# Attention and MLP on one core: key tiles of 128, a shared block-diagonal tile of 64, and row-tiled AV for the rest keys

## The chip, the cores and the metric

The kernel runs on one core of one Trainium2 chip. The metric is the device time of one execution in microseconds (us); a figure for a kernel is the median of its runs.

Engines are named as the profile names them: PE is TensorE (PEld its weight loads; PEq, SPq and so on are the queues from which an engine takes its instructions), DVE is VectorE, ACT is ScalarE, POOL is GpSimd, SP is SyncE, which issues most DMAs.

## The reference

Attention over 8 batches, 12 heads, 448 positions and head size 64, with RMS-normalised queries and keys, followed by an MLP on the 3584 tokens:

```python
q_n, k_n = rmsnorm(q, g_q), rmsnorm(k, g_k)
scores = (q_n @ k_n.T) / sqrt(64)
attn = softmax(scores)                     # 448 x 448 for each of 96 heads
x = (attn @ v) as [8 * 448, 12 * 64]
h = x @ w_in                               # 768 -> 2048
out = (h * clip(h + 3, 0, 6) / 6) @ w_out  # 2048 -> 768
```

## The kernel before

Two heads make a pair; there are 6 pairs per batch and 48 in all. The program is a list of steps with costs, which a small scheduler puts into a fixed order for each engine. A batch's MLP runs between the attention of the next batch's pairs. Only the first batch has no MLP to fill TensorE with; the *first phase* below is the time until the first MLP matmul.

A pair goes through these stations: loads of k, q and v; squares, a reduction and a reciprocal root (`prep`); scaling into `qks`; a transposition into `kq` and `kp` (`turn`; on TensorE for the first 10 pairs, by DMA later); scores and exponentials (`attend`); AV, the product of the exponentials with v, and its normalisation (`gather`). PSUM is the pool that holds the output tiles of the kernel's matmuls. A head's 448 keys are four tiles of 112:

```python
def heads(src, P):
    b, j = divmod(P, NJ)
    return src[b, 2*j:2*j+2, :, :].rearrange("h (p t) d -> p h (t d)", t=T)   # T = 4, p = 112
# loads: one DMA each for k, q and v of a pair
nc.sync.dma_start(out=vf[0:PT], in_=heads(v, P))

# attend: clusters of two score steps, each two matmuls in half of the array's rows
for t0 in range(0, T, size):                      # size = 1 in the first batch, 2 later
    ...
    nc.tensor.matmul(out=ps[:, a, 0:S], lhsT=kp[rows, c0:c0 + 128], rhs=kq[rows, 1, :], start=True, stop=True)
    ...                                           # then exp on ACT, 112 x 896 values for each step

# gather: 4 query tiles x 2 heads x 4 key tiles of 112
nc.tensor.matmul(out=dst[:, a*E1:(a+1)*E1], lhsT=e[0:PT, t, a, c0:c0 + 128], rhs=va[0:PT, a, t, :], ...)

# the start: the loads of g go out on ACT, after q of the first three pairs
g_load = add("ACT", 2.2, 0, load_g, after=1.5, late=3.0)
```

## Time and profile before

| | before |
|---|---|
| median | 442.24 us (441.35 to 443.99, 4 runs; 442.93 in the three runs known to the prediction) |
| span of the profiled run | 438.6 us |
| PE busy | 410.6 us (94%) |
| DVE, ACT, POOL busy | 246.3, 249.0, 240.2 us |
| first score matmul, first MLP matmul | 14.28, 45.48 us |
| DMA packets | 102,923 |

The busy time of each engine in three stretches, in us; the columns are the stretch, its length, the busy us (with the number of instructions) of PE, PEld, DVE, ACT and POOL, then the granted clock (the share of TensorE's full speed that the chip allowed), the DMA share (the time that all packets took over the time of 16 engines; packets overlap, so it can exceed 1) and GB/s:

```profile
10.00:54.60 44.60, 33.78 (x399) 20.31 (x400) 40.39 (x69) 33.38 (x61) 36.84 (x40) 1.00 1.18 250
54.60:106.00 51.40, 50.66 (x508) 28.40 (x509) 37.17 (x59) 37.09 (x65) 38.95 (x35) 1.00 0.96 207
258.00:308.00 50.00, 49.83 (x449) 27.48 (x450) 27.90 (x48) 29.93 (x52) 32.89 (x29) 1.00 0.63 159
```

The clock column has to be read with care at the start: the trace's records of the clock begin at 25.86 us, and before them the column shows 1.00. The matmuls tell otherwise: two score matmuls take 0.56 us at 24.67 us and 0.36 us at 26.27 us.

The chain of work that ended last, followed back from the last instruction through what released each step, as shares of the span by engine, from the page:

```profile
PE 80%; POOL 5%; DVE 4%; ACT 3%; issue 3%; DMA 3%; SPq 1%; POOLq 0%
```

Last, PE's timeline in the steady phase, with start, duration and operation. Durations overlap, so starts are read: the score cluster (S, x4) starts at 263.69 and the next matmul at 264.17, 0.48 us later.

```profile
263.33 0.42 PE L437 MATMUL R<-va,e 112*128 112x65 bf16 x8
263.69 0.55 PE L416 MATMUL S<-kq,kp 64*128 64x448 bf16 x4
264.17 1.15 PE L533 MATMUL M<-xT,w_in_sb 128*128 128x384 bf16 x6
```

### The profile page before, as it was taken

How to read it: one execution, taken by the hardware profiler on the slowest of the kernel's cores; microseconds unless marked ns; L12 is line 12 of the kernel's file. 1: busy time of each engine (PE TensorE's matmuls, PEld its weight loads, DVE VectorE, ACT ScalarE, POOL GpSimd, SP SyncE). 2: the span in 40 equal slices, each digit the busy share in tenths (PEclk: the TensorE clock that was granted, in tenths of full speed). 3: DMA queues.
4: the chain of work that ended last, by engine and by line, in shares of the span. 5: the costliest groups of instructions: out<-in, count | busy, mean ns of one | idle time of the engine just before them, and what ended most of it. 6: DMA issues, size and time to landing. Idle time of an engine off the chain costs nothing.

```text
span 438.6 us, 9205 instructions
## 1 busy us (share of the span) xinstructions
PE 410.6 (94%) x3663; PEld 229.2 (52%) x3682; DVE 246.3 (56%) x417; ACT 249.0 (57%) x425; POOL 240.2 (55%) x230
## 2 busy tenths in 40 slices
PE   0588799999999999999999999999999999999995
PEld 0355455555455565554455565554455555654563
DVE  1998887657674564456555465556564444334421
ACT  3788588657765666367664677357673665123200
POOL 3499988855757567656765657747757510000000
PEclk9999999999999999999999999999999999999999
DMA  8999999877545745674465655684465420220122
GB/s 241 247 265 261 224 214 193 216 197 192 128 121 148 189 113 136 167 214 111 133 156 157 177 135 145 159 214 109 120 161 164 97 56 12 54 81 0 37 72 73
DMA packets 102923, 64.58 MB, mean 147 GB/s; under 512 B 59744, under 2 KB 99424, under 8 KB 102880
## 3 DMA queue, kind: packets, MB, share of 16 engines
q1 hardware_dynamic: 94544, 57.01, 50.6%
q0 software_dynamic: 7296, 6.29, 9.1%
q10 hardware_dynamic: 1040, 0.69, 0.5%
q8 instruction: 29, 0.48, 0.5%
q14 instruction: 14, 0.11, 0.1%
HBM read 45.61 MB, written 11.01 MB: 129 GB/s over the span
## 4 chain that ended last, share of the span: by engine, by line
PE 80%; POOL 5%; DVE 4%; ACT 3%; issue 3%; DMA 3%; SPq 1%; POOLq 0%
PE M L558 27%; PE M L533 25%; PE S L416 9%; PE X L437 8%; PE S L558 4%; PE R L437 2%; PE S L533 2%; DVE ssq L337 1%; ACT e L421 1%; POOL qks L351 1%; PE X L558 1%; POOL sq L322 1%; POOL va L359 1%; DMA gq_t<-in_g_q_dram 1%; POOL sq L329 1%
## 5 line engine op out<-in xcount | busy, mean ns | idle before, releaser
L421 ACT ACTIVATE e<-S 112x896 bf16<-112x896 f32 x192 | 166.3, 914 | 64.1 <-PE S L416 64.0
L533 PE MATMUL M<-xT,w_in_sb 128*128 128x384 bf16 (+1 forms) x679 | 145.1, 349 | 3.7 <-DVE gT L541 2.9
L351 POOL TENSOR_TENSOR qks<-qk,rs 112x512 bf16<-112x512 f32 x87 | 90.5, 1055 | 86.6 <-ACT rs L344 84.7
L558 PE MATMUL M<-w_out_sb,gT 128*128 128x384 bf16 x736 | 131.8, 326 | 0.0
L558 PEld LDWEIGHTS <-gT 128*128 128x128 bf16 x896 | 82.9, 98 | 57.8 <-issue 7.8
L533 PEld LDWEIGHTS <-w_in_sb 128*128 128x128 bf16 x768 | 69.6, 97 | 67.4 <-issue 12.5
L541 DVE SCALAR_TENSOR_TENSOR gT<-t,M 128x384 bf16<-128x384 f32 (+1 forms) x116 | 70.6, 611 | 59.1 <-ACT t L539 58.3
L539 ACT ACTIVATE t<-M 128x384 f32<-128x384 f32 (+1 forms) x116 | 62.6, 540 | 67.0 <-PE M L533 65.5
L437 PEld LDWEIGHTS <-e 112*128 112x128 bf16 x1536 | 65.1, 99 | 31.4 <-issue 16.0
L337 DVE TENSOR_REDUCE ssq<-sq 112x16 f32<-112x1024 f32 (+1 forms) x49 | 58.4, 1193 | 23.3 <-POOL sq L329 12.2
L329 POOL TENSOR_TENSOR sq<-qk 112x1024 f32<-112x1024 f32 x36 | 68.1, 1892 | 0.0
L416 PE MATMUL S<-kq,kp 64*128 64x448 bf16 x384 | 56.6, 364 | 4.1 <-DVE kp L381 1.7
L437 PE MATMUL X<-va,e 112*128 112x65 bf16 x1152 | 58.6, 196 | 0.8 <-ACT e L421 0.6
L566 DVE COPY y<-M 128x384 f32<-128x384 f32 x46 | 25.6, 556 | 59.2 <-PE M L558 59.0
L359 POOL CAST va<-vf 112x512 bf16<-112x512 f32 x48 | 31.5, 658 | 10.4 <-DMA vf<-in_v_dram 10.1
L392 POOL TENSOR_SCALAR kp<-kq,gp 128x448 bf16<-128x448 bf16 x23 | 32.3, 1402 | 5.3 <-DMA kq<-qks 5.2
L463 DVE TENSOR_TENSOR xn<-X,rd 128x384 bf16<-128x384 f32 x48 | 26.8, 558 | 1.6
L416 PEld LDWEIGHTS <-kp 64*128 64x128 bf16 x384 | 12.2, 94 | 27.7 <-issue 18.0
L437 PE MATMUL R<-va,e 112*128 112x65 bf16 x384 | 20.4, 195 | 0.0
L377 PE MATMUL M<-ident,qks 112*128 112x112 bf16 x80 | 7.9, 242 | 13.0 <-DVE qks L351 12.4
L558 PE MATMUL S<-w_out_sb,gT 128*128 128x384 bf16 x112 | 19.5, 326 | 0.0
L462 DVE RECIPROCAL rd<-X 128x6 f32<-128x6 f32 x48 | 9.2, 192 | 15.3 <-PE X L437 15.2
(42 smaller groups left out, 156.2 us busy)
## 6 DMA issues: line engine op xcount, KB each, us to landing
qk<-in_k_dram SPq DMA_DIRECT2D x48, 224.0 KB, 3.3
vf<-in_v_dram SPq DMA_DIRECT2D x48, 224.0 KB, 3.7
qk<-in_q_dram SPq DMA_DIRECT2D x45, 224.0 KB, 3.4
w_in_sb<-in_moe_w_in_dram POOLq DMA_DIRECT2D x4, 768.0 KB, 11.3
w_out_sb<-in_moe_w_out_dram POOLq DMA_DIRECT2D x4, 768.0 KB, 11.9
out_dram<-y SPq DMA_DIRECT2D x8, 336.0 KB, 3.1
out_dram<-y SPq DMA_DIRECT2D x8, 288.0 KB, 3.4
out_dram<-y SPq DMA_DIRECT2D x8, 240.0 KB, 3.2
```

The source lines that it names most:

```text
L329: parts = [add("POOL", 1.93, at - 10, lambda: nc.gpsimd.tensor_tensor(out=sq[0:PT], in0=qk[0:PT], in1=qk[0:PT], op=MULT), *ld, *war, lock= ...
L337: red = add("DVE", 0.6 * n, at - 8 * hurry + 0.5 * i0, lambda i0=i0, i1=i1, cs=cs: nc.vector.tensor_reduce(out=ssq[0:PT, cs], in_=sq[0:PT, ...
L351: sc.append(add(on, 0, at - 6 * hurry, lambda e, i=i, rs4=rs4: engines[e].tensor_tensor(out=qks[0:PT, i].rearrange("p t h d -> p h t d"), ...
L359: vc = add({"POOL": 0.61}, 0, at - 3, lambda e: engines[e].tensor_copy(out=va[0:PT, :, :, 0:D], in_=vf[0:PT].rearrange("p h (t d) -> p h t ...
L392: nc.vector if e == "DVE" else nc.gpsimd).tensor_scalar_mul(
L416: nc.tensor.matmul(out=ps[:, a, 0:S], lhsT=kp[rows, c0:c0 + 128], rhs=kq[rows, 1, :], start=True, stop=True)
L421: x = add("ACT", 0.93, at + step * (t0 + i) / T + 0.2, lambda t=t0 + i, ps=ps: nc.scalar.activation(out=e[0:PT, t], in_=ps[0:PT, :, 0:S], ...
L437: nc.tensor.matmul(out=dst[:, a * E1:(a + 1) * E1], lhsT=e[0:PT, t, a, c0:c0 + 128], rhs=va[0:PT, a, t, :], start=(first and a == 0 and t ...
L533: nc.tensor.matmul(out=m[:, 0:n], lhsT=w_in_sb[:, kt, f * 128:(f + 1) * 128], rhs=X[:, kt, :], start=(kt == 0), stop=(kt == NKT - 1))
L539: r = add("ACT", 0.08 + n / 1200, due + span, lambda: nc.scalar.activation(out=t[:, 0:n], in_=m[:, 0:n], func=RELU, bias=0.5, scale=1.0 / ...
L541: g = add("DVE", 0.12 + n / 960, due + span, lambda: nc.vector.scalar_tensor_tensor(out=G[:, f, :], in0=t[:, 0:n], scalar=1.0, in1=m[:, 0: ...
L558: nc.tensor.matmul(out=m[:, 0:HALF], lhsT=G[:, f, i * 128:(i + 1) * 128], rhs=w_out_sb[:, f, cols], start=(f == 0), stop=(f == NFT - 1))
```

## The change

The intent is to take work off TensorE. Each head's keys become three tiles of 128 and a rest of 64. The rest keys of both heads lie in one tile of 128 rows (head 0 in the upper half, head 1 in the lower), scaled into a block-diagonal tile, so that one matmul in the full array gives the scores of both heads. From the second batch on two pairs share seven score steps instead of eight. The AV of the rest keys runs in row tiles (64 rows for each head, each head in a part of its own of the PSUM tile `X`) inside a score cluster, and the other AV matmuls fall from 64 to 48 for two pairs. The g loads also go out first. The core of the diff:

```diff
+    K7 = 2 * NS + 1                                     # NS = 3: tiles of 2 heads, and the rest tile
+    def load_tiled(e, at, tile_, src, P, war, cost, after):
+        x = heads(src, P)
+        most = add(e, 0.47, at, lambda: engine.dma_start(
+            out=tile_[:, 0:2 * NS].rearrange("p (h t) d -> p h (t d)", h=2),
+            in_=x[:, 0:SM].rearrange("h (p t) d -> p h (t d)", t=NS)), ...)
+        rest = add(e, 0.47, at, lambda: engine.dma_start(
+            out=tile_[:, 2 * NS], in_=x[:, SM:S]), ...)  # 2 heads x 64 rows of 256 bytes
+        return [most, rest]
 ...
+        def scale_rest():                                # makes the tile block diagonal
+            nc.vector.scalar_tensor_tensor(
+                out=qks[:, NS].rearrange("p (h d) -> p h d", h=2),
+                in0=kf[:, 2 * NS].unsqueeze(1).to_broadcast([128, 2, D]),
+                scalar=rs[:, 2 * NS:2 * NS + 1], in1=head[:], op0=MULT, op1=MULT)
 ...
+                    nc.tensor.matmul(                    # rest keys of AV, in row tiles
+                        out=X[:, a, s * E1:(s + 1) * E1], lhsT=er[rows, i, c0:c0 + 128], rhs=va[rows, 2 * NS, :],
+                        start=(s == 0), stop=False, skip_group_check=True)
 ...
+            for cluster, extra, x in (                   # two pairs, seven steps
+                    ([[(P, NS), (P + 1, NS)]], None, POS[0]),
+                    ([[(P, 2)], [(P + 1, 0)]], (0, P), POS[1]),
+                    ([[(P + 1, 1)], [(P + 1, 2)]], None, POS[2])):
 ...
-    g_load = add("ACT", 2.2, 0, load_g, after=1.5, late=3.0)
+    g_load = add("ACT", 1.95, -99, load_g, after=0.7, late=1.0)
```

Since a shared step needs the keys of the second pair early, `EARLY = 0.7` also moves the preparation of every second pair forward by 0.7 of a pair, from the second batch on.

## The prediction

> **What bounds the kernel now.** TensorE, from about 45 us on. The page's busy table gives PE 410.6 of 438.6 us (94%), and the table by windows gives 49.1 to 49.8 busy us in each stretch of 50 between 158 and 358, clock 1.00. The chain of waits is 80% PE; ACT (57%), DVE (56%) and POOL (55%) are off it there. Before that PE waits, while DVE is busy 40.4 of 44.6 us and POOL 36.8 (windows, 10 to 54.6). The first score matmul starts only at 14.28 us: ACT issues g loads until 8.89 us, although the first keys landed at about 4.2 (timeline, chain).
>
> **What a pair costs PE now** (timeline, start to start, 240 to 275 us). A cluster of two score steps, four matmuls, takes 0.483 us until the next full-array matmul; the change into it adds 0.09 (last AV chunk 0.353 before scores, 0.265 otherwise). [...] Two pairs: 4 x 0.573 for scores, 8 AV chunks x 0.265, together 4.41 us.
>
> **What the change does to that.** Two pairs get three row-tiled clusters (3 x 0.573 = 1.72) and one block-diagonal step of two matmuls in the full array (0.38[...]): scores go from 2.29 to 2.10. AV keeps 48 full matmuls at 0.033 (1.59) and adds 16 row-tiled ones inside existing clusters: 0.26 us if the halves run fully abreast, 0.53 if each costs what it does now; I estimate 0.4. Sum 4.09 against 4.41: 0.32 us per two pairs, 21 times, is 6.7 us (4 to 9.5). All of it is on the critical path.
>
> **The start.** The g loads go out first, q of pair 0 moves to SP. ACT should square at about 5 us and the first scores start at about 10. Afterwards DVE and POOL set the pace with about the same work (reduce 15 instead of 16 groups, key scale 0.55 + 0.26 instead of 0.69, kp 512 instead of 448 columns), so I expect the first MLP matmul at about 42 instead of 45.5 us: 3.5 us (0 to 5).
>
> **What it adds.** k and v take two DMAs each, one with 256-byte rows: 384 packets instead of 224, two more SP issues per pair (0.31 to 0.47 us each; SP has room). kp on POOL grows from 1.40 to about 1.6 us, squares and scales shrink. A score cluster now also waits for X to be free and for the rest keys' exponential: a small new risk of PE stalls, say 0 to 3 us, 0.5 expected.
>
> **Prediction.** 442.9 - 6.7 - 3.5 + 0.5: about 433 us, range 428 to 438.5. Faster by over 2%: 0.58; within 2%: 0.40; slower: 0.02.
>
> **What would show each step.** Score clusters without rest keys still 0.48 us, the block-diagonal pair 0.38 without a gap on either side; clusters with rest keys 0.13 to 0.26 longer. ACT e instructions 168 or so of full size instead of 192. First score at 9 to 11 us, first MLP matmul at 41 to 43. PE busy per 50 us unchanged at 49.5 or more.
>
> **What would make it wrong.** Row-tiled AV matmuls that don't overlap, or wait for weight loads (gain 4 us or less); PE gaps at clusters for X or the rest exponential; a start that DMA packets hold, so that nothing is gained before 45 us; or, the other way, fuller overlap and a faster first phase (428).

The forecast's sum came to 442.9 - 6.7 - 3.5 + 0.5 = 433.2 us. The 0.38 us of the block-diagonal step was the author's estimate. The trace of before gives the same: 16 matmuls of 384 columns in the full array take 2.60 us there (265.16 to 267.76 us), so by that rate two of 448 columns take 0.38.

## More of the kernel before

From the page of the kernel before, the busy shares in 40 equal slices of the span (a 9 is 90% or more):

```profile
PE   0588799999999999999999999999999999999995
DVE  1998887657674564456555465556564444334421
ACT  3788588657765666367664677357673665123200
POOL 3499988855757567656765657747757510000000
DMA  8999999877545745674465655684465420220122
```

There are two regimes. In the first five slices DVE, POOL and the DMA engines are nearly full (once they have started) and PE is not. From the sixth slice on PE is full and all others have room.

## The result, and the profile after

The kernel after takes 470.38 us (median of 4 runs, 468.27 to 473.82) against 442.24, and is correct. The ratio is 1.0639, with a 95% interval from 1.0563 to 1.0714. Ratios here and below are the mean time of one kernel's runs over that of the other's of the same rounds, so they are not quite the ratio of the medians.

The busy slices from the page of after:

```profile
PE   0762767669977999999998999999999999999996
DVE  3574874453664757586567667765765554424421
POOL 3465564489547567655385745674656300000000
DMA  5996979998977757865866697898747412120032
```

The loss is at the left: PE is only full from the fourteenth slice on (about 150 us), and in the early slices neither DVE nor POOL is full any more. The stretches that answer to those of before:

```profile
10.00:54.60 44.60, 25.09 (x268) 15.66 (x266) 29.74 (x55) 22.77 (x41) 27.87 (x33) 0.89 0.89 187
54.60:106.00 51.40, 35.15 (x336) 20.74 (x337) 29.28 (x57) 24.56 (x49) 29.21 (x33) 0.90 0.99 166
258.00:308.00 50.00, 49.73 (x476) 29.64 (x474) 34.06 (x60) 28.77 (x51) 29.58 (x34) 1.00 0.79 168
```

In the first stretch every engine does less than before, and the DMA engines too: a share of 0.89 at 187 GB/s instead of 1.18 at 250 GB/s. So the work is short of data, although not more bytes are wanted (45.61 MB are read from HBM in both). The chain says what it waits for; DMA has gone from 3% to 17% and SP's own queue from 1% to 6%:

```profile
PE 58%; DMA 17%; DVE 8%; SPq 6%; POOL 5%; issue 4%; ACT 1%; POOLq 0%; DVEq 0%
```

SP's timeline shows those issues; start, duration, and the load. In the first 40 us of before, an issue took 0.31 to 0.47 us nearly always:

```profile
16.27 0.31 SPq L302 DMA_DIRECT2D qk<-in_k_dram  x1
16.68 0.43 SPq L302 DMA_DIRECT2D qk<-in_q_dram  x1
17.16 0.45 SPq L306 DMA_DIRECT2D vf<-in_v_dram  x1
```

Now SP is stuck in some for 2.4 to 3.5 us, and the issues that begin in the first 60 us take 56.6 us in all, against 17.2 us before. SP is full:

```profile
8.36 2.45 SPq L320 DMA_DIRECT2D kf<-in_k_dram  x1
10.85 0.52 SPq L323 DMA_DIRECT2D kf<-in_k_dram  x1
...
13.27 3.16 SPq L320 DMA_DIRECT2D kf<-in_k_dram  x1
16.48 0.52 SPq L323 DMA_DIRECT2D kf<-in_k_dram  x1
17.05 3.29 SPq L334 DMA_DIRECT2D qf<-in_q_dram  x1
```

TensorE's own part of the change, on the other hand, did what it should. From PE's timeline of after:

```profile
266.17 0.81 PE L683 MATMUL M<-w_out_sb,gT 128*128 128x384 bf16 x4
266.82 0.54 PE L498 MATMUL S<-kq,kp 128*128 128x448 bf16 x2
267.20 0.81 PE L683 MATMUL M<-w_out_sb,gT 128*128 128x384 bf16 x4
...
270.74 0.55 PE L493 MATMUL S<-kq,kp 64*128 64x448 bf16 x4
271.12 0.28 PE L466 MATMUL X<-va,er 64*128 64x65 bf16 x8
271.34 2.12 PE L683 MATMUL M<-w_out_sb,gT 128*128 128x384 bf16 x12
```

The block-diagonal step takes 0.38 us (266.82 to 267.20) with no gap. A cluster with the eight rest-key matmuls takes 0.60 us (270.74 to 271.34), 0.12 more than the 0.48 of a plain one. One check of the prediction was missed here, "PE busy per 50 us unchanged at 49.5 or more": from 160 to 358 us PE waits 3.3 us for DVE's `gT`, and 0.6 us in before.

### The profile page after: what moved, and what is told of

It is laid out like the page before. It is cut to its first block, busy times and chain, and to the rows that moved or that the text cites. A ratio compares the mean times of both kernels' runs of the same rounds, so it can differ in the third digit from the quotient of the medians.

```text
span 472.0 us, 9411 instructions
## 1 busy us (share of the span) xinstructions
PE 410.2 (87%) x3617; PEld 234.2 (50%) x3634; DVE 268.0 (57%) x488; ACT 231.4 (49%) x404; POOL 225.2 (48%) x264
## 3 DMA queue, kind: packets, MB, share of 16 engines
HBM read 45.61 MB, written 11.01 MB: 120 GB/s over the span
## 4 chain that ended last, share of the span: by engine, by line
PE 58%; DMA 17%; DVE 8%; SPq 6%; POOL 5%; issue 4%; ACT 1%; POOLq 0%; DVEq 0%
PE M L683 20%; PE M L658 17%; DMA vf<-in_v_dram 6%; DMA kq<-qks 6%; PE X L578 5%; PE S L493 4%; PE S L683 4%; DMA kf<-in_k_dram 3%; SPq L320 3%; DMA qf<-in_q_dram 2%; POOL sq L352 2%; PE S L658 2%; DVE gT L666 2%; PE X L683 2%; DVE qks L389 2%
## 5 line engine op out<-in xcount | busy, mean ns | idle before, releaser
L526 ACT ACTIVATE e<-S 128x896 bf16<-128x896 f32 x144 | 125.2, 914 | 55.1 <-PE S L493 54.9
L683 PEld LDWEIGHTS <-gT 128*128 128x128 bf16 x896 | 83.3, 98 | 53.4 <-issue 2.0
L368 DVE TENSOR_REDUCE ssq<-sq 128x15 f32<-128x960 f32 (+2 forms) x49 | 55.1, 1127 | 35.0 <-POOL sq L352 27.2
L411 POOL CAST va<-vf 128x448 bf16<-128x448 f32 x48 | 27.5, 573 | 86.5 <-PE X L578 55.6
L578 PEld LDWEIGHTS <-e 128*128 128x128 bf16 x1152 | 55.3, 101 | 22.7 <-issue 3.8
L578 PE MATMUL X<-va,e 128*128 128x65 bf16 x1152 | 61.2, 199 | 0.0
L352 POOL TENSOR_TENSOR sq<-kf 128x448 f32<-128x448 f32 x42 | 39.2, 934 | 20.4 <-DMA kf<-in_k_dram 12.6
L352 POOL TENSOR_TENSOR sq<-qf 112x512 f32<-112x512 f32 x44 | 45.8, 1041 | 4.4 <-DMA qf<-in_q_dram 4.3
L382 POOL TENSOR_TENSOR qks<-kf,rs 128x384 bf16<-128x384 f32 x43 | 37.0, 860 | 18.8 <-ACT rs L375 16.7
L395 POOL TENSOR_TENSOR qks<-qf,rs 112x512 bf16<-112x512 f32 x43 | 45.5, 1058 | 0.0
L389 DVE SCALAR_TENSOR_TENSOR qks<-kf,rs,head 128x128 bf16<-128x128 f32 x48 | 29.7, 633 | 7.4 <-ACT e L526 5.0
```

Source lines behind the costliest of these rows:

```text
L352: engines[e].tensor_tensor(out=o, in0=x, in1=x, op=MULT)
L368: lambda i0=i0, i1=i1, rows=rows: nc.vector.tensor_reduce(out=ssq[0:rows, i0:i1], in_=sq[0:rows, i0:i1], axis=AX_X, op=ADD),
L382: engines[e].tensor_tensor(out=qks[:, 0:NS].rearrange("p t (h d) -> p h t d", h=2), in0=kf[:, 0:2 * NS].rearrange("p (h t) d -> p h t d", ...
L389: nc.vector.scalar_tensor_tensor(out=qks[:, NS].rearrange("p (h d) -> p h d", h=2), in0=kf[:, 2 * NS].unsqueeze(1).to_broadcast([128, 2, D ...
L395: engines[e].tensor_tensor(out=qks[0:PT, 4:4 + T].rearrange("p t (h d) -> p h t d", h=2), in0=qf[0:PT].rearrange("p (h t) d -> p h t d", h=2),
L526: lambda dst=dst, ps=ps, w=2 if whole else 1: nc.scalar.activation(out=dst, in_=ps[:, 0:w, 0:S], func=EXP), s, *(AVW[P] if t < NS else AVR ...
```

## The experiments

Eighteen kernels ran, in this order of argument. "First MLP" is the start of the first MLP matmul in the profiled run: 45.5 us before, 60.5 after. All medians of before lie between 441.9 and 443.4 us.

One caution holds for all of them. The scheduler plans anew when a cost or a step changes. By the traces every engine keeps its order of work from after to e2, e6 and e7, from e3 to e4, from e9 to e16 and from before to e17, the added dummy matmuls aside. In all other comparisons the order changed too, so what they show is an edit with its new order, not the edit alone.

| run | median us | ratio to before (95%) | first MLP |
|---|---|---|---|
| after | 470.4 | 1.064 (1.056 to 1.071) | 60.5 |
| e1 | 474.3 | 1.073 (1.068 to 1.078) | 54.7 |
| e2 | 453.1 | 1.028 (1.021 to 1.035) | 53.9 |
| e3 | 470.7 | 1.064 (1.060 to 1.068) | 57.7 |
| e4 | 452.0 | 1.022 (1.018 to 1.025) | 51.9 |
| e5 | 453.9 | 1.023 (1.019 to 1.028) | 54.4 |
| e6 | 451.6 | 1.020 (1.017 to 1.024) | 53.6 |
| e7 | 451.5 | 1.020 (1.017 to 1.024) | 54.2 |
| e8 | 444.4 | 1.002 (0.998 to 1.006) | 45.5 |
| e9 | 448.9 | 1.013 (1.009 to 1.018) | 58.4 |
| e10 | 443.4 | 0.999 (0.996 to 1.002) | 54.8 |
| e11 | 469.3 | 1.059 (1.056 to 1.061) | 68.0 |
| e12 | 451.6 | 1.018 (1.016 to 1.021) | 53.0 |
| e13 | 450.9 | 1.020 (1.016 to 1.024) | 53.6 |
| e14 | 455.1 | 1.027 (1.021 to 1.033) | 58.0 |
| e15 | 448.1 | 1.014 (1.011 to 1.017) | 47.4 |
| e16 | 451.6 | 1.017 (1.010 to 1.023) | 57.1 |
| e17 | 450.7 | 1.018 (1.015 to 1.021) | 53.4 |
| e18 | 444.6 | 1.007 (1.003 to 1.011) | 52.3 |

e2, e5, e6 and e10 give a wrong result (they load other rows). e14 gave one that was not intended. All others are correct.

### Theory and rivals

The rest DMA reads `x[:, SM:S]`, whose outermost dimension is the two heads. The traces show two things about such a DMA. Landings: before's trace holds 4832 landing events for its 302 DMAs, 16 for each, and after's 5120 for 398, which is 302 times 16 and 96 times 3; 96 is the number of rest DMAs. Packets: in the first 40 us of after, no more than four of the 1664 packets of 256 bytes, which are the rest rows, are ever under way at once, while of the 768-byte packets of the same keys and values up to 21 are. How many DMA engines carry a rest DMA is not shown. *Theory A* is therefore that rest DMAs of this shape move few packets at a time and hold up the loads behind them. *Rival B* is the larger number of packets and issues, whatever their shape. *Rival C* is work on DVE and POOL, the new scale of the rest keys above all. (The expectations name it theory D; their theory C is the number of issues on SP in e1 to e4, and the clock in e16 and e17.)

### e1: the rest DMA split by head

```diff
-        rest = add(..., out=tile_[:, 2 * NS], in_=x[:, SM:S])
+        rest = [add(..., out=tile_[h * 64:(h + 1) * 64, 2 * NS], in_=x[h, SM:S]) for h in range(2)]
```

> Theory A: each DMA for the rest keys names its source as 2 heads x 64 rows[...]. Split in one DMA per head (64 rows each), the same bytes and packets[...]: 428 to 437 us, first MLP matmul near 42 us instead of 60. Theory B, the number and smallness of packets: no change, 465 us or more. Theory C, too many DMA issues on SP's queue: slower than the changed kernel, as two more are issued per pair.

It took 474.33 us, no better than after, so theory A's number was missed. The long issues are gone, but each pair of rest DMAs now takes 1.1 us to issue, and from 17.94 us on there is a stretch in which the issues follow one another with hardly a gap:

```profile
16.37 0.37 SPq L320 DMA_DIRECT2D kf<-in_k_dram  x1
17.94 1.10 SPq L323 DMA_DIRECT2D kf<-in_k_dram  x2
19.09 0.59 SPq L335 DMA_DIRECT2D qf<-in_q_dram  x1
19.73 0.46 SPq L320 DMA_DIRECT2D vf<-in_v_dram  x1
20.23 1.11 SPq L323 DMA_DIRECT2D vf<-in_v_dram  x2
21.47 0.66 SPq L320 DMA_DIRECT2D kf<-in_k_dram  x1
```

The experiment changed three things at once, the landings (all its DMAs have 16), issues and the order, and decides nothing about A. Nor does it show that SP is the new limit: the issues that begin in the first 60 us take 41.3 us, SP waits for landings in between, and SP's queue has 5% of the chain. The first MLP matmul comes 5.8 us earlier than in after and the total is no better. Why e1 is slow stays open.

### e2: the rest DMA reads 128 consecutive rows

```diff
-            out=tile_[:, 2 * NS], in_=x[:, SM:S])
+            out=tile_[:, 2 * NS], in_=x.rearrange("h s d -> (h s) d")[SM:SM + 128, :])
```

> Wrong result on purpose: the rest DMA reads 128 consecutive rows instead of the last 64 rows of each of two heads; everything else, the number of DMAs, packets, bytes and issues too, is as in the changed kernel. Theory A: 428 to 437 us, as in e1, and 16 completions per DMA. Theories B and C: as the changed kernel, 465 to 475 us.

The bytes, packets and issues are as many, and only the shape differs (the result is wrong, since the rows are others). It took 453.07 us: 17 us of the 28 us are gone, but not all: theory A's 428 to 437 us was missed by 16 us, and so was the 465 to 475 us of B and C. Here, as in e7 below, every DMA has its 16 landings again.

### e3 and e4: the same loads added to the kernel before

e3 adds two unused DMAs of 2 x 64 rows for each pair to the kernel before; e4 adds the same bytes from 128 consecutive rows:

```diff
+        for src, due in ((k, at - 26), (v, at - 19)):
+            dx, war, use = dx_r.take()
+            use.append(add("SP", 0.47, due, lambda src=src, dx=dx: nc.sync.dma_start(
+                out=dx[:], in_=heads_of(src)[:, SM:S]), ...))                       # e3
+                out=dx[:], in_=heads_of(src).rearrange("h s d -> (h s) d")[SM:SM + 128, :]), ...))  # e4
 ...
```

> The kernel before, with two extra DMAs per pair of the shape that the change added (2 heads x 64 rows of 256 bytes into an unused tile). Theory A: 458 to 480 us, with most of the loss before 160 us. Theory B and C: slower too, by the same amount as e4.

> As e3, but the extra DMAs read 128 consecutive rows: same bytes, packets and issues. Theory A: 442 to 448 us. Theory B or C: as e3, 455 us or more.

e3 took 470.65 us and e4 451.96. e3 is within theory A's forecast; e4 lies between A's (442 to 448) and that of B and C (455 or more). e3 has the 5120 landings of after. The shape alone costs 18.7 us in the kernel before as well, about what e2 gained, and the order of work is the same on both sides of each comparison. Together these two pairs of runs show theory A, with its size. e4 costs 9.7 us for 64 KB more per pair, together with a new order: the first phase of before takes little more load, though how much of the 9.7 us is the order is not shown.

### e5 and e6: fewer packets and issues

e5 loads k and v with one DMA each of 128 packets of 1792 bytes; e6 with two even DMAs, 256 packets. Both give a wrong result.

```diff
-            out=tile_[:, 0:2 * NS]..., in_=x[:, 0:SM]...)
-        rest = add(...)
+            out=tile_[:], in_=x.rearrange("h s d -> (h s) d").rearrange("(p t) d -> p t d", t=K7))   # e5
```

> Wrong result on purpose: k and v by one DMA each of 128 packets of 1792 bytes. Packets and issues theory alike: 426 to 436 us, first MLP matmul at about 42 us, that is, what was predicted for the change. PE-side theory: 450 or more.

> Wrong result on purpose: k and v by two DMAs each as in e2, but each partition reads 7 consecutive rows, as 1024 and 768 bytes: 256 packets instead of 384 for the same bytes, same number of issues, order unchanged. If the 10 us that e2 still loses are packets: 430 to 440 us. If they are the two further issues per pair: as e2, 450 or more. If they come from the PE side or the order of instructions: 450 or more here and in e5.

453.85 and 451.62 us: no better than e2. So with the shape mended, rival B was not what limited the first phase, and the expected 426 to 440 us was missed by far. The outcome is that of the last branch, "450 or more here and in e5". e6 is the cleaner of the two, since its order is that of e2.

### e7: a correct layout with adjacent rest rows

Which 64 keys of a head are its rest does not matter for the result. If head 0 gives its last 64 rows and head 1 its first 64, the rest is 128 consecutive rows of memory:

```diff
-            in_=x[:, 0:SM].rearrange("h (p t) d -> p h (t d)", t=NS))
+            in_=bass.AP(x.tensor, x.offset, [[NS * D, 128], [(S + 64) * D, 2], [1, NS * D]]))
-            out=tile_[:, 2 * NS], in_=x[:, SM:S])
+            out=tile_[:, 2 * NS], in_=x.rearrange("h s d -> (h s) d")[SM:SM + 128, :])
```

> Right result: head 0 keeps its last 64 rows as rest, head 1 its first 64, which lie next to each other, so the rest DMA is 128 consecutive rows[...], with no further issue or packet. Theory A: 452 us, as e2 (450 to 456). If e2 was fast because of its wrong data, this one is at 470.

It is correct and takes 451.46 us, as theory A expected. The same number of issues on SP, in the same order, now takes 29.8 us of the first 60 instead of the 56.6 of after. In the packet records, the 70,400 packets of 256 bytes take 1936 us in all in after and 1596 us here, for the same bytes. The loss that remains is about 9 us, and its first stretch now looks quite different from that of after:

```profile
10.00:54.60 44.60, 29.59 (x333) 18.46 (x333) 41.07 (x65) 25.05 (x45) 33.36 (x39) 0.77 1.12 237
```

DMA has 1.12 again, DVE is full (41.07 of 44.6), and PE waits.

### e8: only the earlier g loads

The part of the change that concerns the start, alone in the kernel before:

```diff
-    g_load = add("ACT", 2.2, 0, load_g, after=1.5, late=3.0)
+    g_load = add("ACT", 1.95, -99, load_g, after=0.7, late=1.0)
-            e = "ACT" if i and P < 3 else "SP"
+            e = "ACT" if i and 0 < P < 3 else "SP"
```

> The kernel before with the start of the change alone: g loads first on ACT's queue, q of pair 0 on SP's. My prediction gave the start 3.5 us: 437 to 441 us. If the first 45 us are set by the DMA engines and not by the first score: 442 to 444, no gain.

The first score came at 12.24 instead of 14.28 us, but the first MLP matmul at 45.46, as before, and the time was 444.41 us. An earlier start gains nothing, so the latency of the first pair does not set the end of the first phase. That the amount of work sets it is argued from the busy times. The 3.5 us of the prediction were not there in this kernel.

### e12: the rest scale alone, in the kernel before

```diff
+        extra = add("DVE", 0.26, at - 9 * hurry, lambda: nc.vector.scalar_tensor_tensor(
+            out=dz[0:PT], in0=qk[0:PT, 0, 0, 0:D].unsqueeze(1).to_broadcast([PT, 2, D]),
+            scalar=rs[0:PT, 0:1], in1=head[0:PT], op0=MULT, op1=MULT), r, head_make, lock=True)
 ...
```

> The kernel before with one extra DVE instruction per pair of the same kind (two SBUF inputs, 112 x 128 elements, result unused). Theory D: first MLP matmul 4 to 8 us later than 45.5, 447 to 452 us. If DVE has room: 442 to 444.

451.57 us: one unused instruction per pair costs 8.2 us, as theory D expected. The instruction's own time is only a part of that: seven ran before the first MLP matmul and took 4.3 us together, and that matmul comes 7.5 us later. The rest is the new order, or work that waits behind the instruction; the two were not separated. It is a DVE instruction with two SBUF inputs, planned at 0.26 us. In after it is L389; the view of that line gives the shortest, the median and the longest duration in ns:

```profile
L389 DVE SCALAR_TENSOR_TENSOR qks<-kf,rs,head x48: 335/356/2117, 8.7 to 366.7; 128x128 bf16<-128x128 f32 x48
```

At its shortest it takes 0.34 us, but it averages 0.63 (29.7 us for 48). Before the first MLP matmul nine of them take 5.2 us in after and 8.2 us in e7. What stretches it is not shown: a pair of them took 2.38 us on DVE at 26.97 us (2.12 us of it the first),

```profile
26.97 2.38 DVE L389 SCALAR_TENSOR_TENSOR qks<-kf,rs,head 128x128 bf16<-128x128 f32 x2
```

just while POOL worked from 26.47 on:

```profile
26.47 0.55 POOL L411 CAST va<-vf 128x448 bf16<-128x448 f32 x1
26.97 0.88 POOL L298 DMA_DIRECT2D w_in_sb<-in_moe_w_in_dram  x1
27.88 1.06 POOL L395 TENSOR_TENSOR qks<-qf,rs 112x512 bf16<-112x512 f32 x1
```

From 27.02 to 27.88 us, however, POOL only issued a DMA, and the L389 at 43.72 us took 0.34 us although POOL was in a tensor operation from 43.20 to 44.74; what held DVE at 26.97 is open.

### e9, e10 and e11: the rest scale on ScalarE

```diff
-            nc.vector.scalar_tensor_tensor(out=qks[:, NS]..., in1=head[:], ...)
+            for a in range(2):
+                rows = slice(a * 64, a * 64 + 64)
+                nc.scalar.activation(out=qks[rows, NS, a * 64:(a + 1) * 64], in_=kf[rows, 2 * NS],
+                                     func=COPY, scale=rs[rows, 2 * NS:2 * NS + 1])
 ...
```

e9 does this in e7, e10 in e5 (one load each, wrong result), e11 in after.

> Right result: e7, and the scale of the rest keys goes from one DVE instruction with two SBUF inputs (0.34 us when quiet, up to 2.5 us[...], 8.2 us before the first MLP matmul in e7) to two ACT instructions on a half each; the zeros of the block diagonal are set once. Theory D: the rest of the loss, 9 us in e7, comes from that DVE instruction, as DVE is busy all of the first 54 us: first MLP matmul at 45 to 49 us, 438 to 445 us. If it is the order of the steps or the PE side: 449 to 453 as e7.

> Wrong result on purpose (e5's loads): one DMA each for k and v of 128 packets, and the rest scale on ACT. If packets and issues come to matter once DVE is relieved: 5 us or more below e9. If not: within 3 us of e9.

> The changed kernel with its rest DMAs[...] as they are, rest scale on ACT alone. [...]466 to 472, hardly better than the changed kernel. If the two causes simply add: about 460.

The same edit gains 10.5 us from e5 to e10, 2.5 us from e7 to e9, and 1 us in after; the last two are within the spread of the runs (the intervals of the ratios overlap). Theory D's forecast for e9 was missed, in the total (438 to 445) and more so in the first MLP matmul: it was to come at 45 to 49 us and came at 58.4, later than the 54.2 of e7. In e11 it came 7.5 us later than in after. e10 and e11 went as expected (for e11, 466 to 472 us was expected if the rest DMAs bind by themselves; it took 469.3). Effects in the first phase do not add: the reading that fits is that an engine that is relieved helps only where no other is full, and that in after the rest DMAs with 3 landings hide it almost wholly. Packets and issues, too, count once DVE is relieved: e10 is 5.6 us faster than e9, where e5 was no faster than e7. Rival B was wrong as the cause of the whole loss, and right as a part of it, as far as the new orders of these runs allow it to be said.

e10 also shows the gain on TensorE in the total. From the first DMA transposition of gathered rest tokens (at 70.35 us before, 80.36 in e10) to the end of the last matmuls (about 434.2 and 437.5) it takes 357.1 us instead of 363.9. That is 6.7 us less, as predicted. The exact agreement is partly luck, since it depends on the mark: from the end of the 18th pair's normalisation (`xn` on DVE) to the last matmul, with about 15 of the 21 shared blocks, it is 300.8 us instead of 305.2, 4.4 us where 15 x 0.32 = 4.8 was predicted. All of the gain is spent by the 10 us that the first phase takes longer.

### e13: sharing only from the third batch on

What still held the first phase up in e9 and e10 was open. Theory L: sharing needs the preparation of one pair more before the first MLP. Theory P: DVE and POOL have too much to do in any order. e13 is e9 without sharing in the second batch:

```diff
-        if P < NJ:
+        if P < 2 * NJ:
             blocks.append((begin[P], lambda P=P: attend_first(P)))
 ...
```

> The kernel with adjacent rest rows and the rest scale on ScalarE, where the second batch of clusters shares nothing (three clusters per pair) and two pairs share their steps only from the third batch on, so that keys of pairs 6 and 7 need not be ready before the first MLP. Theory L (the first MLP comes late because sharing needs one pair more of preparation before the gather of pair 5): first MLP matmul at 54 us or earlier (58.4 without), total 444 or less. Theory P (VectorE and GpSimd have too much to do in the first phase in any order): first MLP at 57 to 60 us, total 447 to 452. The second batch itself costs about 1 us more of TensorE time.

The first MLP matmul came at 53.6 instead of 58.4 us, as L expected, but the total was 450.9 us, as P expected. What was gained had been given back by 90 us. e18 follows that up.

### e14 and e15: squares on ScalarE

Both move the squares of pairs 3 to 9 (of queries too, not of keys alone as the expectations say) from DVE and POOL to ACT, e14 in e9, e15 in before:

```diff
-            on = {"ACT": 0.63} if P < 3 else {"DVE": 0.68, "POOL": 1.04}
+            on = {"ACT": 0.63} if P < NPE else {"DVE": 0.68, "POOL": 1.04}
```

> The kernel with adjacent rest rows and the rest scale on ScalarE, and the squares of the keys of pairs 0 to 9 on ScalarE too, instead of VectorE and GpSimd. Theory P (work of VectorE and GpSimd[...] limits the first phase): first MLP matmul at 50 us or earlier, total 436 to 443, so it could beat the kernel before. Theory L (order of preparation): first MLP within 2 us of 58, total 446 to 451. If ScalarE becomes the limit: later than 58 and above 450.

> Control: the kernel before, with the squares of the keys of pairs 0 to 9 on ScalarE. Theory P: first MLP matmul before 43 us (45.5 without) and total 436 to 441. Theory L says nothing of it: 441 to 444. If ScalarE becomes the limit of the first phase: 443 or more.

e15 took 448.14 us, its first MLP matmul at 47.4 us. ACT is then nearly full from 20 to 50 us (8.91, 9.24 and 9.29 of each 10 us), so ScalarE has no room either, the third case of the expectation. e14 took 455.08 us. Its result was wrong (relative error 0.166), although it differs from the correct e9 only in where squares run and in the order that follows; the reason was not found, and nothing is built on this run.

### e16 and e17: dummy matmuls to hold the clock up

The sharing kernels show a low granted TensorE clock in the first phase: from 10 to 54.6 us it is 0.77 to 0.89 in after, e1, e2, e5, e7, e9, e10, e13 and e18, where before has 1.00. So do kernels that do not share: it is 0.89 in e4 and 0.92 in e8 and e12, 0.94, 0.84 and 0.88 in each 10 us from 20 to 50 us in e15, and over whole runs 0.958 to 0.974 in e3, 0.991 to 1.000 in before. In e9 the stretch from 34 to 38 us had exactly half (the columns as above). It began at 32.64 us and lasted 6.83 us; the longest idle time of PE just before was 2.35 us:

```profile
30.00:34.00 4.00, 1.65 (x12) 0.80 (x11) 3.97 (x5) 1.44 (x3) 3.27 (x4) 0.83 1.16 192
34.00:38.00 4.00, 3.79 (x45) 2.35 (x44) 3.86 (x8) 3.54 (x9) 2.21 (x3) 0.50 1.06 287
```

What lowers the clock is not shown. Does the low clock cost time? *Theory C* says so. e16 puts 12 dummy matmuls ahead of each group of TensorE transposes of e9; e17 does it in before.

```diff
+                    if i == 0:
+                        for _ in range(WARM):            # 12
+                            nc.tensor.matmul(out=m[:, 0:128], lhsT=ident[:], rhs=ident[:], start=True, stop=True,
+                                             skip_group_check=True)
 ...
```

> The kernel with adjacent rest rows and the rest scale on ScalarE (448.9 us), with 12 dummy matmuls of 128 columns ahead of each group of TensorE transposes of the first 10 pairs and of the first batch's outputs (16 groups, about 0.67 us each at the full clock, 10.7 us in all); they write to the PSUM tile that the transposes then overwrite, and wait for nothing but that tile. Every engine keeps its order. Theory C ([...]0.50 to 0.83 in the windows from 30 to 60 us, and that costs about 9 us): granted clock at least 0.95 from 20 to 60 us, first MLP matmul at 52 us or earlier (58.4), total 438 to 444. Rival, no effect of the clock because VectorE sets the pace: clock up all the same, first MLP within 2 us of 58, total 447 to 452.

> Control: the same dummy matmuls in the kernel before, whose clock is 1.00 from 10 to 60 us anyway. Theory C: nothing to gain, 442 to 447, since the dummies cost up to 5 us where TensorE is not waiting. If it gains more than 2 us, dummies help in another way than by the clock.

From 30 to 60 us the clock of e16 was 1.00 (0.66 to 0.81 in each 10 us of e9), yet the first MLP matmul came only 1.3 us earlier (57.1) and the total was 451.6 us. From 20 to 30 us the clock was still 0.66, so "at least 0.95" was met from 30 us on only. As it stands this is the outcome of the rival, that the clock has no effect. But the control does not allow that conclusion. e17 took 450.7 us, 7.6 more than before and above the 442 to 447 that were expected, with the first MLP matmul 8 us later, although its dummies need only about 10.7 us in all (an estimate of 16 groups at 0.67 us; in e17 the group at 26.97 us takes 0.68 at clock 1.00, the one at 17.19 takes 1.26), PE is idle for more than that in the first phase, and every engine kept its order. So dummies in front of the transposes are not free: TensorE's order is tight there too. (Nor is it a pure control: its clock fell to 0.70 from 50 to 60 us, and the 1.00 that was expected of before holds from 25.86 us on only.) If they cost as much in e16, the full clock has gained some of it back. In e9 PE was busy for 3.79 of the 4 us at half clock above, so the low clock was not only a sign of waits. What is shown is that these dummies and the clock together bring nothing; what the clock alone costs stays open.

### e18: two pairs more transposed on TensorE

In e13 the chain of waits runs through one piece after the first MLP matmul (start, duration, what):

```profile
61.49 0.93 POOL sq L349
62.42 0.28 POOL w_out_sb L300
62.70 13.89 DMA kq<-qks
76.59 0.02 issue
76.61 0.35 DVE kp L441
76.97 1.06 DVE ssq L365
```

This is the first DMA transposition, of pair 10. It was issued at 62.70 and landed 13.89 us later; the median of its kind is 3.3 us. The DMA share was 1.24 from 62 to 66 us. DVE waited 6.1 us for it, with MLP work queued behind, and PE behind DVE. e9 loses about 5 us at the same place in another way (POOL, too, waits there once for a DMA transposition, 6.3 us). ACT stands idle for 5.20 us in front of a rest scale,

```profile
74.87 0.48 ACT L661 ACTIVATE t<-M 128x384 f32<-128x384 f32 x1
80.55 0.70 ACT L388 ACTIVATE qks<-kf,rs 64x64 bf16<-64x64 f32 x2 [5.20 <-issue]
```

for which the profile names no releaser. SP was busy with the issue of a DMA transposition out of `qks` from 75.36 to 80.23, so a wait for a free `qks` buffer is the likely reason; it is inferred, not shown. e18 is e13 with the transpositions of 12 pairs on TensorE:

```diff
-    NPE = 10
+    NPE = 12
```

> The kernel that shares from the third batch on (450.9 us, first MLP matmul at 53.6), with the queries and keys of 12 pairs instead of 10 transposed on TensorE. Theory T (the 4.8 us that the first MLP came earlier were given back because the first DMA transposition of scores' operands landed 13.9 us after its issue, behind loads in a full queue, and VectorE waited 6.1 us for it, ScalarE and TensorE behind it): no wait for a landing of a DMA transposition above 3 us before 110 us, TensorE busy above 46 us of 50 from 60 to 110 us (42.5 without), total 444 to 447. If the loads themselves hold the first phase up and the transposition only shows it: total 449 to 453, with another wait of 4 us or more for a load between 60 and 110 us.

It took 444.6 us, is correct, and PE is busy 47.23 of 50 us from 60 to 110, instead of 42.48 in e13. No wait for a DMA transposition is left in the list of waits there, on any engine. First e13, then e18:

```profile
60.00:110.00 50.00, 42.48 (x441) 25.18 (x440) 27.36 (x53) 32.79 (x67) 34.47 (x38) 0.97 0.91 181
```

```profile
60.00:110.00 50.00, 47.23 (x514) 28.38 (x512) 32.47 (x62) 36.77 (x72) 37.14 (x41) 1.00 0.88 189
```

All that was expected came in. This fits the reading that e13 had lost in that one transposition what it gained in the first phase; the new order of e18 came with it, so the two are not separated.

e18 is the best correct version of the change, and it does not beat the kernel before: the ratio is 1.0068, with an interval from 1.0029 to 1.0106. Whether 12 pairs on TensorE would help the kernel before was not run.

## Why the prediction was right or wrong

The prediction was 433 us, with a range of 428 to 438.5; the result was 470.4.

**TensorE's saving: right.** Clusters still take 0.48 us, the block-diagonal step 0.38 without a gap, and a cluster with rest keys 0.12 more, just under the predicted 0.13 to 0.26. The full-array step shows no gap on either side, while the change into a cluster costs 0.09 us in before (its last AV chunk 0.353 us instead of 0.265); what happens in that change was not shown. The saving is there: 6.7 us in e10 by one mark, 4.4 of 4.8 us by the other.

**The loads: the step that failed.** The prediction said: "k and v take two DMAs each, one with 256-byte rows: 384 packets instead of 224, two more SP issues per pair (0.31 to 0.47 us each; SP has room)." It counted bytes, packets and issues and set 0.5 us for all that is added. It did not look at the shape of the source. With the outer dimension of 2 each rest DMA had 3 landings instead of 16, and in the first 40 us of after no more than four of the rest rows' packets were under way at once. That shape costs 17 to 19 us (after to e2 and e7; e3 against e4), where the term was 0.5 us. "SP has room" failed with it: SP was stuck in single issues for 2.4 to 3.5 us, and its issues took 56.6 of the first 60 us. The count was not at fault: the same number of issues takes 29.8 us in e7.

**"DVE and POOL set the pace with about the same work": wrong.** The sum of planned costs was about the same, but the new rest scale took 0.63 us on the mean instead of 0.26, and in before DVE was already busy 40.4 of 44.6 us. In after itself DVE is busy 29.7 us only, and the loads set the pace; the rest scale comes to bear once these are mended (e7: 41.1 us). Adding the instruction to the kernel before, with a new order, costs 8.2 us (e12). Taking it off DVE, again with a new order, gains 10.5 us in e10 and an unclear 2.5 us in e9. That it is a cause of the 9 us that remain is likely; its share is not shown.

**The start: wrong.** The first score came at 12.1 us, not 9 to 11, and the two us that it came earlier bring nothing (e8).

**The slack that was assumed for the first phase: wrong.** In before DVE (40.4 of 44.6 us), POOL (36.8) and the DMA engines are nearly full there, and TensorE's order is tight. Small additions to before cost 9.7 us on DMA (e4), 8.2 on DVE (e12), 7.6 on PE (e17), and shifting squares to ACT costs 6 (e15). Only e17 kept the order, and e8, with a new order too, cost nothing clear of noise. That this lack of slack is the common root is argued, not shown.

The difference between the kernel after and its best version can be followed in steps: adjacent rest rows gain 19 us (470.4 to 451.5), the rest scale on ScalarE 2.5 (448.9, within the spread), no sharing in the second batch loses 2 (450.9, within the spread of these runs) and 12 pairs on TensorE gain 6.3 (444.6). The steps do not add in another order, as e10 and e11 show.

**What stays open.** In e18 the first MLP matmul still comes at 52.3 us, 6.8 us later than before. How that divides between packets (e10 against e9 suggests several us), the order of preparation (4.8 us between e9 and e13) and the rest was not settled, and neither was what the low clock costs. A test that keeps the order of before fixed and adds only the rest scale was not run. Why e1 is slow and why e14's result is wrong is open too.

## What to carry to other kernels

Ask of a change where its cost falls, not only how large it is: this one saves on TensorE where TensorE is the limit and adds to DMA, DVE and SP in the one phase where these are the limit. Read a DMA's outermost dimension before its bytes, and compare its landing events with those of the other DMAs: here an outermost dimension of 2 gave 3 landings where the others had 16, and it cost 18.7 us (e3 against e4). When a repair moves the first milestone and not the total, follow the chain past that milestone; here a DMA transposition of 13.9 us stood there. And where a scheduler plans anew after each edit, compare the orders before an effect is put down to the edit: the clean pairs here are those whose order stayed.
